# Attention steps of 256 queries inside the first MLP, with TensorE held to the source's order from block 1 on

## The chip, the cores and the metric

One NeuronCore of a Trainium2 chip runs the whole kernel. The metric is the device time of one execution in microseconds (us); of the kernel before three executions were timed, and one more was profiled. TensorE (PE in the profile) does the matmuls, VectorE (DVE) and ScalarE (ACT) the element-wise work, and SyncE's queue (SP) issues every DMA.

## What is computed

Chunked attention feeds two MLPs (called "moe" in the reference, with no routing):

```python
# attention: 4 batches, 8 heads, 768 queries, head size 64; per chunk of 32 queries
k_full = concat([mem_k (8), k[c_start-16 : c_end+8]])      # at most 64 keys
scores = q_c @ k_full.T / sqrt(64)
a = exp(scores - max(scores));  a = a / (sum(a) + 1e-9)
out_c = a @ v_full
# MLP 1 on x = out as [3072 tokens, 512]
h = x @ w_in;   y = (h * sigmoid(1.702 * h)) @ w_out        # 512 -> 2048 -> 512
# MLP 2 on y
h = y @ w_in2;  result = (max(h,0) + alpha * min(h,0)) @ w_out2
```

## The kernel before, in words

The 3,072 tokens are cut into 24 **attention steps** of 128 queries (`m` = 0 to 23). One step loads q, k and v (lines 273 to 285), forms the scores on TensorE (`sc`, L295: 32 small matmuls, which the trace counts as 64, in two PSUM banks of which half is used), then does the softmax: the row maximum and the subtraction on VectorE (L316, L324), the exponential on ScalarE (L337), the sum, reciprocal and scaling on VectorE (L343 to L348). Four transposes (`pt`, L358) turn the probabilities, ScalarE copies them out (L363), 32 matmuls with v give the step's output (`xp`, L373, again 64 in the trace), and ScalarE and VectorE split it into a high and a low part of `x` (L387, L388). For `m` in `NACC` (4 to 7) the exponential is eight ScalarE instructions with a running sum (L332) in place of one.

MLP 1 runs over six blocks of 512 tokens, in each over 16 chunks of 128 hidden units. Every product is made of three matmuls on high and low parts. One **MLP step** is `mm1` (L425: 12 matmuls 128x512 into `h`, of which there are two buffers), the activation on ScalarE and VectorE (L433, L434), its split into `gh` and `gl` (L470, L471), and one MLP step later `mm2` (L481: 12 matmuls into the pairs `ya` and `yb`, one buffer each). At a block's end `finish1` copies the four banks out (L490, L492) and stores them. During block 0 the 16 chunks of weights are converted from a 64-bit format (lines 108 to 144: about 4.6 us of VectorE each, and two ScalarE passes). From the sixth MLP step of block 1 on, the weights of MLP 2 are prepared on the side (`prep_place`, lines 192 to 239: per unit four VectorE passes over 1024 columns, four small sums L221, three subtractions L233, and casts on ScalarE).

Steps 0 to 3 run ahead of block 0. Steps 4 to 23 are spread over blocks 0 to 4 by `plan`: step `m` starts at tick `8*(m-4)`; its transposes stand three ticks later, the product with v five. Two ticks belong to an MLP step (`attend`, lines 823 to 826). The four parts of a step share one place of two PSUM banks, tag `"a"`. A scheduler then sorts the instructions of each engine by its own estimate of when they are ready; only those passed to `keep_in_program_order` (`kp`) stay where the source has them. TensorE's MLP 1 and attention instructions are free before the change. An engine takes its instructions one after another in the sorted order. Later stages (MLP 2, L621 and L719) are in fixed order and untouched.

Of the kernel before, what the change touches and what calls it, by code (L numbers as in the profile page):

```python
# [17 lines left out]
QG = 64  # L18
WIN = LEFT + CHUNK + RIGHT
NK = NMEM + LEFT + QG + RIGHT + NMEM  # L20
KW = NMEM + WIN
# [37 lines left out]
def fused_kernel(ctx: ExitStack, tc: tile.TileContext, qs, ks, vs, ident, w_in1, w_out1, w_in2, w_out2, alpha, out):  # L59
# [210 lines left out]
    def pair(tag, name):  # L270
        return ps1.tile([128, 2, DM], F32, tag=tag, name=name)
# [107 lines left out]
    def a_xcopy(m):  # L379
# [7 lines left out]
        nc.scalar.copy(hi, x)  # L387
        nc.vector.tensor_tensor(out=lo, in0=x, in1=hi.bitcast(F32), op=ALU.subtract)  # L388

    plan = {}  # L390
# [28 lines left out]
    def mm1(p, x, n, f):  # L419
        h = ps2.tile([128, TBM], F32, tag="h", name=f"h{p}")  # L420
        wh, wl = wt[p, f]
        i = 0
        for k in range(NKC):
            for w, z in ((wh, 0), (wh, 1), (wl, 0)):
                nc.tensor.matmul(  # L425
                    h[:, :n], w[:, 0, k * 128:(k + 1) * 128], x[:, z, k, :n], start=(i == 0), stop=(i == 3 * NKC - 1)
                )
                i += 1
        return h

# [45 lines left out]
    def mm2_t(p, y, gs, n, f):  # L476
        gh, gl = gs
        wh, wl = wt[p, f]
        for m in range(NKC):
            for i, (w, g) in enumerate(((wh, gh), (wh, gl), (wl, gh))):  # L480
                nc.tensor.matmul(  # L481
                    y[m][:, :n], w[:, 1, m * 128:(m + 1) * 128], g[:, :n],
                    start=(f == 0 and i == 0), stop=(f == NF - 1 and i == 2),
                )

    def finish1(y, t0, n):
        for m in range(NKC):
# [323 lines left out]
    a_load(NSTART)  # L811
    a_load_v(NSTART)

    def do_mm2(i):
        p, j, t0, n, f = steps[i]
# [98 lines left out]
```

## Time and profile before

| | us |
|---|---|
| median of 3 runs (1100.96 to 1103.57) | 1101.12 |
| the profiled execution, its own time | 1100.41 |
| span of its trace | 1098.6 |
| TensorE busy | 1070.5 (97% of the span) |
| VectorE busy | 766.3 (70%) |
| ScalarE busy | 409.7 (37%) |

Matmuls are pipelined: in a stream of 128x512 matmuls each has a duration of 0.39 us, but the next starts about 0.227 us after it. In what follows a **slot** is that distance from one start to the next, and the cost of something put between two big matmuls is what it adds to the sum of slots.

### The profile page before, as it was taken

What the parts mean: (1) busy time and instruction counts of PE and PEld (TensorE: products, weight loads), DVE (VectorE), ACT (ScalarE), POOL (GpSimd) and SP (SyncE); (2) the same over time, 40 slices, a digit from 0 to 9 for tenths busy, and PEclk for the clock granted to TensorE, in tenths of its full rate; (3) what the DMA queues carried; (4) which work ended last, traced back from release to release, by engine and by line L of the source; (5) the groups of instructions that cost most, each with busy time, mean ns of one, the idle gap of its engine ahead of it and who ended that gap; (6) DMA issues with size and microseconds to landing.
All of it is one profiled execution on the core that took longest, in us unless ns stands there. A gap on an engine that the chain in (4) does not pass through costs nothing.

```text
span 1098.6 us, 18378 instructions
## 1 busy us (share of the span) xinstructions
PE 1070.5 (97%) x7516; PEld 867.9 (79%) x7516; DVE 766.3 (70%) x1090; ACT 409.7 (37%) x633; POOL 0.2 (0%) x4
## 2 busy tenths in 40 slices
PE   5799999999999999999999999999999999999998
PEld 4577778888887887788788888888888888888886
DVE  6899833667676767766652257898777888677965
ACT  2566523334434434434432222245222345122442
POOL 0000000000000000000000000000000000000000
PEclk6699999999999999999999999999999999999999
DMA  8763522446646554665432066676666867666661
GB/s 292 261 202 125 158 84 64 151 170 217 219 165 208 192 194 151 222 215 177 158 130 67 1 194 197 210 268 207 201 199 199 296 200 216 201 187 212 219 203 58
DMA packets 84098, 200.23 MB, mean 182 GB/s; under 512 B 9520, under 2 KB 26288, under 8 KB 84016
## 3 DMA queue, kind: packets, MB, share of 16 engines
q1 hardware_dynamic: 84016, 199.07, 55.7%
q8 instruction: 59, 0.97, 0.4%
q14 instruction: 23, 0.19, 0.1%
HBM read 157.10 MB, written 41.94 MB: 181 GB/s over the span
## 4 chain that ended last, share of the span: by engine, by line
PE 87%; DVE 6%; DMA 3%; ACT 2%; issue 1%; SPq 0%; DVEq 0%; ACTq 0%
PE h L425 21%; PE accx L719 15%; PE accx L621 12%; PE ya L481 11%; PE yb L481 10%; PE accy L719 6%; PE accy L621 6%; PE hz L621 3%; PE xp L373 2%; DMA wraw<-w_out 2%; PE sc L295 1%; DVE wtmp L127 1%; DVE wtmp L124 1%; PE pt L358 1%; DMA y<-o 1%
## 5 line engine op out<-in xcount | busy, mean ns | idle before, releaser
L425 PE MATMUL h<-x,whi 128*128 128x512 f32 x768 | 246.0, 396 | 3.8 <-ACT whi L137 1.8
L425 PEld LDWEIGHTS h<-x,whi 128*128 128x128 f32 x768 | 143.6, 189 | 36.3 <-ACT whi L137 2.6
L434 DVE SCALAR_TENSOR_TENSOR t<-t,h 128x512 f32<-128x512 f32 x96 | 65.8, 685 | 125.8 <-ACT t L433 125.6
L425 PE MATMUL h<-x,wlo 128*128 128x512 f32 x384 | 152.0, 396 | 0.0
L433 ACT ACTIVATE t<-h 128x512 f32<-128x512 f32 x96 | 57.6, 600 | 162.8 <-PE h L425 162.6
L719 PE MATMUL accx<-r,u 128*128 128x512 f32 x360 | 86.5, 395 | 0.0
L621 PE MATMUL accx<-xw,u 128*128 128x512 f32 x240 | 85.7, 390 | 0.2 <-ACT u L604 0.2
L425 PEld LDWEIGHTS h<-x,wlo 128*128 128x128 f32 x384 | 72.4, 188 | 15.6 <-DVE wlo L142 0.4
L719 PE MATMUL accx<-rx,u 128*128 128x512 f32 x360 | 84.6, 390 | 0.0
L471 DVE TENSOR_TENSOR gl<-t,gh 128x512 fp32r<-128x512 f32 x96 | 65.8, 686 | 23.0 <-ACT gh L470 21.8
L719 PEld LDWEIGHTS accx<-r,u 128*128 128x128 f32 x360 | 67.5, 187 | 16.3
L719 PEld LDWEIGHTS accx<-rx,u 128*128 128x128 f32 x360 | 67.3, 188 | 15.0 <-DVE rx L674 0.5
L470 ACT CAST gh<-t 128x512 fp32r<-128x512 f32 x96 | 59.7, 622 | 45.9 <-DVE t L434 41.6
L481 PE MATMUL ya<-gh,whi 128*128 128x512 f32 x192 | 76.2, 397 | 0.3 <-ACT gh L470 0.3
L481 PE MATMUL ya<-gl,whi 128*128 128x512 f32 x192 | 76.3, 397 | 0.0
L481 PE MATMUL yb<-gl,whi 128*128 128x512 f32 x192 | 75.3, 392 | 0.0
L481 PE MATMUL yb<-gh,wlo 128*128 128x512 f32 x192 | 75.3, 392 | 0.0
L481 PE MATMUL yb<-gh,whi 128*128 128x512 f32 x192 | 75.1, 391 | 0.0
L481 PE MATMUL ya<-gh,wlo 128*128 128x512 f32 x192 | 75.1, 391 | 0.0
L604 ACT COPY s<-accx 128x512 f32<-128x512 f32 x24 | 14.1, 589 | 148.4 <-PE accx L621 148.4
L670 ACT CAST rx<-g 128x1024 fp32r<-128x1024 f32 x42 | 44.4, 1057 | 64.7 <-DVE g L454 24.3
L621 PE MATMUL accx<-xh,u 128*128 128x512 f32 x192 | 66.9, 389 | 0.0
(130 smaller groups left out, 1818.4 us busy)
## 6 DMA issues: line engine op xcount, KB each, us to landing
u<-wo SPq DMA_DIRECT2D x84, 512.0 KB, 4.7
u<-wi SPq DMA_DIRECT2D x72, 512.0 KB, 4.2
v<-vs SPq DMA_DIRECT2D x24, 512.0 KB, 4.3
k<-ks SPq DMA_DIRECT2D x24, 416.0 KB, 5.1
wraw<-w_in SPq DMA_DIRECT2D x16, 512.0 KB, 5.2
wraw<-w_out SPq DMA_DIRECT2D x16, 512.0 KB, 5.8
raw<-w_in SPq DMA_DIRECT2D x32, 256.0 KB, 3.6
wi<-ob SPq DMA_DIRECT2D x16, 512.0 KB, 4.0
```

Source lines behind the costliest of these rows:

```text
L124: nc.vector.scalar_tensor_tensor(out=a, in0=top, scalar=0xC0000000, in1=a, op0=ALU.bitwise_and, op1=ALU.bitwise_or)
L373: nc.tensor.matmul(x[half[z], g, j, c * CHUNK:(c + 1) * CHUNK], s["v"][half[g], c, 2 * j + z, :], s["p"][half[g], 2 * z + j // 2, b * CHUN ...
L425: nc.tensor.matmul(h[:, :n], w[:, 0, k * 128:(k + 1) * 128], x[:, z, k, :n], start=(i == 0), stop=(i == 3 * NKC - 1))
L433: mark["s"] = nc.scalar.activation(out=t[:, :n], in_=h[:, :n], func=AF.Tanh, scale=1.702 / 2).ins
L434: mark["v"] = nc.vector.scalar_tensor_tensor(out=t[:, :n], in0=t[:, :n], scalar=1.0, in1=h[:, :n], op0=ALU.add, op1=ALU.mult).ins
L470: mark["s"] = nc.scalar.copy(gh[:, :n], g[:, :n]).ins
L471: mark["v"] = lo_eng.tensor_tensor(out=gl[:, :n], in0=g[:, :n], in1=gh[:, :n].bitcast(F32), op=ALU.subtract).ins
L481: nc.tensor.matmul(y[m][:, :n], w[:, 1, m * 128:(m + 1) * 128], g[:, :n], start=(f == 0 and i == 0), stop=(f == NF - 1 and i == 2),)
L604: kp(nc.scalar.copy(t, src))
L621: kp(nc.tensor.matmul(to, w[:, c, k * 128:(k + 1) * 128], x[:, k], start=(i == 0 and n not in ADDED), stop=(i == 5), skip_group_check=n in ...
L670: kp(nc.scalar.copy(ring[P, d, jj][0], src))
L719: kp(nc.tensor.matmul(to[:, m], w[:, ft, c, m * 128:(m + 1) * 128], g[:, ft], start=(jj == 0 and ft == 0 and i == 0 and n not in ADDED), s ...
```

## The change

From step 4 on, two steps are taken together (`m` = 4, 6, ... 22): ten double steps of 256 queries with functions of their own, `d_load` to `d_xcopy`. Scores, transposed probabilities and outputs now fill both banks of the place `"a"`. The row maximum, subtraction, sum, scaling and the copy of the probabilities work on 1024 columns at once; the exponential for `m` in `NACC` (now 4 and 6) is 16 ScalarE instructions. The three loads are twice as large and are planned together five ticks ahead. The probabilities `p` share the SBUF place of q (tag `qp`) and the exponentials that of k (tag `ke`), one buffer each. A double step starts every 16 ticks, transposes five ticks and the product with v eight ticks after the start. From the first step of block 1 on, `pe()` keeps TensorE's instructions of MLP 1 and attention in the source's order.

```diff
+    def pe(i):
+        if pinned:
+            tc.keep_in_program_order(i)
...
+    def d_load(m):
+        q = ap["pool"].tile([128, 2, 2, 2, HP, CHUNK], F32, tag="qp", name=f"q{m}")
+        nc.sync.dma_start(out=q.rearrange("p s g c j q -> p s (g c j q)"), in_=qs[m:m + 2].rearrange("s p n -> p s n"))
+        k = ap["pool"].tile([128, 2, 2, HP, NK], F32, tag="ke", name=f"k{m}")
+        nc.sync.dma_start(out=k.rearrange("p s g j n -> p s (g j n)"), in_=ks[m:m + 2].rearrange("s p n -> p s n"))
+        v = ap["pool"].tile([128, 2, 2, H, D], F32, tag="v", name=f"v{m}")
+        nc.sync.dma_start(out=v.rearrange("p s c h d -> p s (c h d)"), in_=vs[m:m + 2].rearrange("s p n -> p s n"))
...
+        nc.vector.tensor_reduce(out=mx, in_=flat(sc), axis=mybir.AxisListType.X, op=ALU.max)
...
+        nc.vector.tensor_tensor(out=flat(ex), in0=flat(sc), in1=over(mx), op=ALU.subtract)
...
+            for i in range(DW):
+                nc.scalar.activation(
+                    out=ex[:, i], in_=sc[:, i], func=AF.Exp, scale=1.0 / D ** 0.5,
+                    bias=t["nmx"][:, i:i + 1], accum_out=sm[:, i:i + 1],
+                )
...
+        nc.vector.tensor_tensor(out=ex, in0=ex, in1=over(sm), op=ALU.mult)
...
+        t["p"] = ap["pool"].tile([128, 2, 4, 128], F32, tag="qp", name=f"p{m}")
...
-    for m in range(NSTART, NSG):
+    for m in range(NSTART, NSG, 2):
         b = 8 * (m - NSTART)
         if m > NSTART:
-            at(b - 7, a_load, m)
-            at(b - 2, a_load_v, m)
-        at(b, a_scores, m)
-        at(b, a_max, m)
-        at(b, a_exp, m)
-        at(b + 1, a_norm, m)
-        at(b + 3, a_trans, m)
-        at(b + 3, a_pcopy, m)
-        at(b + 5, a_pv, m)
-        at(b + 5, a_xcopy, m)
-    done_tick = lambda m: 0 if m < NSTART else 8 * (m - NSTART) + 6
+            at(b - 5, d_load, m)
+        at(b, d_scores, m)
+        at(b, d_max, m)
+        at(b, d_exp, m)
+        at(b + 2, d_norm, m)
+        at(b + 5, d_trans, m)
+        at(b + 5, d_pcopy, m)
+        at(b + 8, d_pv, m)
+        at(b + 8, d_xcopy, m)
+    done_tick = lambda m: 0 if m < NSTART else 8 * ((m - NSTART) // 2 * 2) + 9
...
-                nc.tensor.matmul(
+                pe(nc.tensor.matmul(
...
+        if i == NF:
+            pinned.append(True)
```

How the change moves instructions, at three places. First **TensorE at the end of block 0 and in block 2**, the scores of a step (`sc`) among the big matmuls (`h` is mm1, `ya` and `yb` are mm2). Before, the scores of step 8, in pieces of 3, 1 and 28:

```order
L425 MATMUL h_1614<-x_738,wlo_0_339 128x512
L295 MATMUL sc_1660<-k_1440,q_1438 32x64 x3
L481 MATMUL ya<-gh,whi_15_1353 128x512
L481 MATMUL yb<-gh,whi_15_1353 128x512
L295 MATMUL sc_1660<-k_1440,q_1438 32x64
L481 MATMUL ya<-gl,whi_15_1353 128x512
```

In the change, the scores of the double step 12 (L417), between a whole mm1 (now L545) and a whole mm2 (now L601):

```order
L545 MATMUL h_2628<-x_1970,whi_3_667 128x512 x2
L545 MATMUL h_2628<-x_1970,wlo_3_668 128x512
L417 MATMUL sc_2650<-k_2549,q_2547 32x64 x64
L601 MATMUL ya<-gh,whi_2_545 128x512
L601 MATMUL ya<-gl,whi_2_545 128x512
L601 MATMUL ya<-gh,wlo_2_546 128x512
```

In blocks 1 to 5 TensorE now alternates 12 matmuls of mm1 and 12 of mm2, and each part of a double step stands in one piece between two of these groups; in each of the eight double steps there, two mm1 and two mm2 stand between the scores and the transposes.

Second, **VectorE in block 2**, the softmax of step 12 among the activation (`t`, `gl`) and the preparation (`oa`, `ob`). Before:

```order
L316 TENSOR_REDUCE mx_2670<-sc_2635 128x8
L324 TENSOR_TENSOR ex_2671<-sc_2635,mx_2670 128x512
L434 SCALAR_TENSOR_TENSOR t<-t,h_2676 128x512
L233 TENSOR_TENSOR ob_2_2594<-ob_2_2594 128x2x256
L233 TENSOR_TENSOR ob_2_2595<-ob_2_2595 128x2x256
L343 TENSOR_REDUCE sm_2674<-ex_2671 128x8
L471 TENSOR_TENSOR gl<-t,gh 128x512
L346 TENSOR_SCALAR sm_2674<-sm_2674 128x8
L347 RECIPROCAL sm_2674<-sm_2674 128x8
L348 TENSOR_TENSOR ex_2671<-ex_2671,sm_2674 128x512
```

In the change (L441 is the maximum, L446 the subtraction, L466 the sum, L469 the scaling, L554 and L591 the activation):

```order
L441 TENSOR_REDUCE mx_2717<-sc_2650 128x16
L446 TENSOR_TENSOR ex_2718<-sc_2650,mx_2717 128x1024
L466 TENSOR_REDUCE sm_2721<-ex_2718 128x16
L554 SCALAR_TENSOR_TENSOR t<-t,h_2750 128x512
L233 TENSOR_TENSOR oa_2577<-oa_2577 128x3x256
L467 TENSOR_SCALAR sm_2721<-sm_2721 128x16
L591 TENSOR_TENSOR gl<-t,gh 128x512
L233 TENSOR_TENSOR ob_3_2728<-ob_3_2728 128x2x256
L233 TENSOR_TENSOR ob_3_2729<-ob_3_2729 128x2x256
L468 RECIPROCAL sm_2721<-sm_2721 128x16
L469 TENSOR_TENSOR ex_2718<-ex_2718,sm_2721 128x1024
L554 SCALAR_TENSOR_TENSOR t<-t,h_2791 128x512
```

The softmax instructions are half as many and twice as wide, and the three subtractions of the preparation (L233) and one whole activation stand between the sum and the scaling.

Third, **ScalarE at the start of block 0**: the cast of step 3's output (`x_267<-xp_487`), for which the first mm1 waits, and the exponentials of step 4. Before:

```order
L363 COPY p_485<-pt_480 128x512
L322 ACTIVATE nmx_600<-mx_597 128x8
L332 ACTIVATE ex_598,sm_602<-sc_564,nmx_600 128x64 x8
L387 CAST x_267<-xp_487 128x2x4x64
L110 ACTIVATE wtmp<-wraw_2_329 128x1024
```

In the change:

```order
L363 COPY p_485<-pt_480 128x512
L387 CAST x_267<-xp_487 128x2x4x64
L110 ACTIVATE wtmp<-wraw_2_329 128x1024
L110 ACTIVATE wtmp<-wraw_3_429 128x1024
L444 ACTIVATE nmx_634<-mx_631 128x16
L455 ACTIVATE ex_632,sm_636<-sc_564,nmx_634 128x64 x13
L553 ACTIVATE t<-h_548 128x512
```

The cast now stands ahead of the exponentials, and these ahead of the first activation.

## Rows read from the trace of the kernel before

**Rows 1.** Windows: span, busy of PE, PEld, DVE, ACT, POOL; PEclk, DMA, GB/s

```profile
150.00:250.00 100.00, 100.00 (x970) 80.93 (x948) 56.94 (x95) 35.26 (x58) 0.00 (x0) 1.00 0.39 131
```

**Rows 2.** Timeline of TensorE, step 9 in block 1: start, duration, instruction

```profile
171.20 0.39 PE L425 MATMUL h<-x,wlo 128*128 128x512 f32 x1
...
172.56 0.39 PE L481 MATMUL ya<-gh,wlo 128*128 128x512 f32 x1
172.87 0.86 PE L295 MATMUL sc<-k,q 64*32 64x64 f32 x64
173.66 0.50 PE L481 MATMUL yb<-gh,whi 128*128 128x512 f32 x1
174.00 0.39 PE L481 MATMUL yb<-gl,whi 128*128 128x512 f32 x1
...
182.41 0.39 PE L425 MATMUL h<-x,wlo 128*128 128x512 f32 x1
182.64 0.60 PE L358 MATMUL pt<-id_sb,ex 128*128 128x128 f32 x4
182.99 0.71 PE L425 MATMUL h<-x,whi 128*128 128x512 f32 x2
...
187.86 0.39 PE L425 MATMUL h<-x,whi 128*128 128x512 f32 x1
188.17 1.14 PE L373 MATMUL xp<-p,v 64*64 64x32 f32 x64
189.24 0.50 PE L425 MATMUL h<-x,whi 128*128 128x512 f32 x1
```

**Rows 3.** Timeline of TensorE, a piece of six score matmuls in step 8

```profile
145.78 0.39 PE L425 MATMUL h<-x,wlo 128*128 128x512 f32 x1
146.10 0.31 PE L295 MATMUL sc<-k,q 64*32 64x64 f32 x6
146.34 0.50 PE L481 MATMUL ya<-gh,whi 128*128 128x512 f32 x1
```

**Rows 4.** Waits of TensorE, 150 to 545 us: total us, times, longest

```profile
PE h L425 <- DVE t L434: 0.7, 1, 0.7
PE h L425 <- ACT x L387: 0.7, 1, 0.7
PE h L425 <- DVE x L388: 0.6, 1, 0.6
```

**Rows 5.** Timeline of VectorE, softmax of step 9 (no preparation beside it)

```profile
172.31 0.69 DVE L434 SCALAR_TENSOR_TENSOR t<-t,h 128x512 f32<-128x512 f32 x1 [3.90 <-ACT t L433]
173.69 0.69 DVE L471 TENSOR_TENSOR gl<-t,gh 128x512 fp32r<-128x512 f32 x1 [0.69 <-ACT gh L470]
174.30 0.68 DVE L316 TENSOR_REDUCE mx<-sc 128x8 f32<-128x512 f32 x1
...
176.41 0.69 DVE L343 TENSOR_REDUCE sm<-ex 128x8 f32<-128x512 f32 x1 [0.70 <-ACT ex L337]
...
177.57 0.69 DVE L348 TENSOR_TENSOR ex<-ex,sm 128x512 f32<-128x512 f32 x1
```

**Rows 6.** Groups of instructions on VectorE: busy us, mean ns of one, idle before

```profile
L124 DVE SCALAR_TENSOR_TENSOR wtmp<-wraw,wtmp 128x1024 uint32<-128x1024 uint32 x16 | 19.5, 1218 | 0.0
...
L233 DVE TENSOR_TENSOR oa<-oa 128x768 fp32r<-128x768 f32 x16 | 15.2, 953 | 0.2
...
L221 DVE TENSOR_TENSOR ob<-oa 128x256 f32<-128x256 f32 x32 | 12.1, 418 | 0.0
```

**Rows 7.** Chain of waits: the exponentials of step 4 ahead of block 0

```profile
36.59 2.49 ACT ex L332 x15
```

**Rows 8.** Timeline of TensorE: its longest wait in block 0

```profile
126.81 0.73 PE L425 MATMUL h<-x,whi 128*128 128x512 f32 x2 [1.84 <-ACT whi L137]
```

**Rows 9.** DMA rate over the first 25 us, in 40 slices

```profile
GB/s 0 0 26 210 365 373 370 301 257 218 306 305 357 361 394 403 412 424 403 424 407 396 397 419 402 399 392 393 340 209 131 37 26 92 138 367 229 131 265 365
```

**Rows 10.** Timeline of ScalarE: the last copy out of `yb` at a block's end

```profile
448.77 0.60 ACT L490 ACTIVATE o<-yb 128x512 f32<-128x512 f32 x1 [5.30 <-DMA y<-o]
```

More of the change, by code (lines that the diff above doesn't have):

```diff
@@ L388, in a_xcopy @@
         nc.vector.tensor_tensor(out=lo, in0=x, in1=hi.bitcast(F32), op=ALU.subtract)
+    DW = 2 * HP * 2
+    pinned = []
+    def pe(i):
[8 more added lines that the diff above has]
+        nc.sync.dma_start(out=v.rearrange("p s c h d -> p s (c h d)"), in_=vs[m:m + 2].rearrange("s p n -> p s n"))
+        st[m] = dict(q=q, k=k, v=v)
@@ new lines, in d_scores @@
+    def d_scores(m):
+        t = st[m]
+        sc = pair("a", f"sc{m}").rearrange("p z (s n k) -> p z s n k", s=2, k=KW)
+        for s in range(2):
+            for jh in range(2):
+                for g in range(2):
+                    for c in range(2):
+                        for jp in range(2):
+                            for z in range(2):
+                                pe(nc.tensor.matmul(
+                                    sc[quarter[2 * c + jp], z, s, 2 * jh + g, :], t["q"][half[z], s, g, c, 2 * jh + jp, :],
+                                    t["k"][half[z], s, g, 2 * jh + jp, run[c]], start=True, stop=True,
+                                ))
+        t["sc"] = sc
@@ new lines, in flat, with over, d_max @@
+    def flat(t):
+        return t.rearrange("p z s n k -> p (z s n) k")
+    def over(t):
+        return t.rearrange("p (n k) -> p n k", k=1).to_broadcast([128, DW, KW])
+    def d_max(m):
+        t = st[m]
+        sc = t["sc"]
+        for s in range(2):
+            for g in range(2):
+                for n in (g, 2 + g):
+                    if (2 * (m + s) + g) % GPB == 0:
+                        nc.vector.memset(sc[half[0], :, s, n, NMEM:NMEM + LEFT], NEG)
+                    if (2 * (m + s) + g) % GPB == GPB - 1:
+                        nc.vector.memset(sc[half[1], :, s, n, WIN - RIGHT:WIN], NEG)
+        mx = ap["pool"].tile([128, DW], F32, tag="mx", name=f"mx{m}")
+        t["ex"] = ex = ap["pool"].tile([128, 2, 2, 4, KW], F32, tag="ke", name=f"ex{m}")
+        nc.vector.tensor_reduce(out=mx, in_=flat(sc), axis=mybir.AxisListType.X, op=ALU.max)
+        if m in NACC:
+            t["nmx"] = ap["pool"].tile([128, DW], F32, tag="nmx", name=f"nmx{m}")
+            nc.scalar.mul(t["nmx"], mx, -1.0 / D ** 0.5)
+            return
+        nc.vector.tensor_tensor(out=flat(ex), in0=flat(sc), in1=over(mx), op=ALU.subtract)
@@ new lines, in d_exp @@
+    def d_exp(m):
+        t = st[m]
+        ex = flat(t["ex"])
+        t["sm"] = sm = ap["pool"].tile([128, DW], F32, tag="sm", name=f"sm{m}")
+        if m in NACC:
+            sc = flat(t["sc"])
+            for i in range(DW):
[3 more added lines that the diff above has]
+                )
+            return
+        nc.scalar.activation(out=ex, in_=ex, func=AF.Exp, scale=1.0 / D ** 0.5)
@@ new lines, in d_norm, with d_trans @@
+    def d_norm(m):
+        t = st[m]
+        ex, sm = flat(t["ex"]), t["sm"]
+        if m not in NACC:
+            nc.vector.tensor_reduce(out=sm, in_=ex, axis=mybir.AxisListType.X, op=ALU.add)
+        nc.vector.tensor_scalar(out=sm, in0=sm, scalar1=1e-9, scalar2=None, op0=ALU.add)
+        nc.vector.reciprocal(sm, sm)
+        nc.vector.tensor_tensor(out=ex, in0=ex, in1=over(sm), op=ALU.mult)
+    def d_trans(m):
+        t = st[m]
+        t["pt"] = pt = pair("a", f"pt{m}").rearrange("p s (i q) -> p s i q", q=128)
+        e = t["ex"].rearrange("p z s (j g) k -> p z s j (g k)", g=2)
+        for s in range(2):
+            for i in range(4):
+                pe(nc.tensor.transpose(pt[:, s, i, :], e[:, i // 2, s, i % 2, :], id_sb))
@@ new lines, in d_pcopy, with d_pv @@
+    def d_pcopy(m):
+        t = st[m]
+        t["p"] = ap["pool"].tile([128, 2, 4, 128], F32, tag="qp", name=f"p{m}")
+        nc.scalar.copy(t["p"], t["pt"])
+    def d_pv(m):
+        t = st[m]
+        x = pair("a", f"xp{m}").rearrange("p g (s j q) -> p g s j q", s=2, q=QG)
+        for s in range(2):
+            for j in range(HP):
+                for c in range(2):
+                    b = 2 * c + j % 2
+                    for g in range(2):
+                        for z in range(2):
+                            pe(nc.tensor.matmul(
+                                x[half[z], g, s, j, c * CHUNK:(c + 1) * CHUNK], t["v"][half[g], s, c, 2 * j + z, :],
+                                t["p"][half[g], s, 2 * z + j // 2, b * CHUNK:(b + 1) * CHUNK], start=True, stop=True,
+                            ))
+        t["x"] = x
@@ new lines, in d_xcopy @@
+    def d_xcopy(m):
+        tok = m * SQ
+        b = int(np.searchsorted(p1_start, tok, side="right")) - 1
+        if b not in xt:
+            xt[b] = xp.tile([128, 2, NKC, TBM], F32R, tag=f"x{b % 2}", name=f"x{b}")
+        x = st.pop(m)["x"]
+        for s in range(2):
+            off = tok + s * SQ - int(p1_start[b])
+            hi, lo = [xt[b][:, i, :, off:off + SQ].rearrange("p j (g q) -> p g j q", g=2) for i in range(2)]
+            nc.scalar.copy(hi, x[:, :, s])
+            nc.vector.tensor_tensor(out=lo, in0=x[:, :, s], in1=hi.bitcast(F32), op=ALU.subtract)
@@ L424, in mm1 @@
             for w, z in ((wh, 0), (wh, 1), (wl, 0)):
-                nc.tensor.matmul(
+                pe(nc.tensor.matmul(
                     h[:, :n], w[:, 0, k * 128:(k + 1) * 128], x[:, z, k, :n], start=(i == 0), stop=(i == 3 * NKC - 1)
-                )
+                ))
                 i += 1
```

7 lines of the change are left out of this document (3 added, 4 removed).

## The prediction

> **What bounds the kernel now.** I read the windows by stage first: in block 1 TensorE is busy for all of its 100 us at the full granted clock (1.00, the level of 2.4 GHz), VectorE for 57 and ScalarE for 35 [rows 1]. So in MLP 1 time is saved only by shortening what TensorE does or by removing what it waits for. Then TensorE's timeline, to see what an attention step costs there. A big matmul starts 0.227 us after the one before it. The slot after 172.56 would begin at 172.79; the scores put it off to 173.66, and the matmul after that comes 0.34 us later, not 0.23: 0.87 + 0.11 = 0.98 us for 64 matmuls. The four transposes cost in the same way 182.99 - 182.64 = 0.35, with the 0.11 behind them 0.46; the product with v 189.24 - 188.09 + 0.11 = 1.26 [rows 2]. One step: 2.70 us, two: 5.40. A piece of only six score matmuls costs 146.34 - 146.01 + 0.11 = 0.44 [rows 3]. So 58 further matmuls cost 0.54 us, 9 ns each, and a piece has a fixed part of 0.44 - 6 x 0.009 = 0.38 us. That is what larger steps can save. Last the waits: between 150 and 545 us TensorE waits only three times, 2.0 us in all [rows 4].
>
> The sum is made against the profiled execution, 1100.41 us; the median of the runs shown lies 0.71 above it.
>
> **Blocks 1 to 4, larger pieces: -8.0 us.** Eight double steps. Scores 0.98 + 64 x 0.009 = 1.56; transposes with the same fixed part 0.38 + 2 x 0.08 = 0.54; product with v 0.38 + 2 x 0.88 = 2.14. Together 4.24, which saves 1.16 us per double step. If only the 0.11 behind a piece were fixed, three pieces less would save 0.33. I take 1.0, near the first, because the piece of six is measured for the scores alone: 8 x 1.0, bounds 2.6 and 9.3.
>
> The Trainium skill states in "TensorE: Matmul & The Clock Gate", section "Wait — 56ns, not 53.3ns?", that start to start never falls below about 25 ns, however small a matmul is. The trace disagrees for these matmuls (9 ns each), and the measurement decides. By the rule the 128 matmuls added to scores and output would cost an estimated 3.2 us instead of 1.5, a double step some 6.0 in place of 5.4, and this term would be +4.6.
>
> **Source order, no cut pieces: -1.9 us.** Before, the scores of steps 8, 12 and 16 are cut into three, two and three pieces; five pieces less by 0.38.
>
> **Source order, waits of before: -2.0 us.** The three waits [rows 4] come from mm1 matmuls that the scheduler put ahead of what they need, two of them at the start of block 5, where `x` came late. In source order the last product with v of a block stands two MLP steps ahead of the block's end, so `x` is there. Bounds 0 and 2.6, the latter if the slow restart after a wait goes too.
>
> **Source order, waits at the transposes: +9.3 us.** This is the term that eats the others. From the scores' end TensorE has two mm1 and two mm2 before the transposes: 48 slots, 10.9 us. In that time VectorE must finish a softmax twice as wide, among the instructions that the scheduler puts between. I count from the end of the slot of the last mm1 matmul (t = 0; at 171.43 in step 9). The activation's VectorE part starts at 0.88, `gl` at 2.26 [rows 5]. Queued instructions of 0.69 us start 0.61 apart [rows 5], so a pass over 1024 columns, 1.22 alone [rows 6], counts 1.13 in a queue and 1.25 where the next one needs its result. The exponential takes about 0.70 of the 2.11 us between maximum and sum [rows 5]; twice as wide I estimate 1.1.
>
> Step 12, as the order of the change has it: activation 0.88 to 1.48, a preparation pass to 2.61, `gl` to 3.2, four L221 (0.42 alone [rows 6], 0.35 in a queue) with two memsets to 4.8, maximum 6.05, subtraction 7.3, exponential 8.4, sum 9.55, next activation 10.15, the wide L233 (0.95 [rows 6]) 11.05, the small addition 11.25, `gl` 11.85, two L233 of 0.6 each 13.05, reciprocal 13.25, scaling 14.5; transposes at 14.65. TensorE gets there at 1.6 + 0.1 + 10.9 = 12.6. It waits 2.1 us. The same count gives 1.5 for step 14, 2.1 for 16 and for 18 (two preparation passes between), 0.6 for 20 and 0.9 for 22. Steps 8 and 10, with little or no preparation beside them, are ready at 9.5 to 11: no wait. Sum 9.3. Bounds: 0, if the preparation falls elsewhere (step 9 alone took 178.26 - 174.30 = 4 us from maximum to scaling, twice as wide it would be under 7), and 14, if each of the six waits is 0.8 us longer. `gl` is late too, but needed only behind the transposes; the copy of `p` and the product with v come 8.2 us after the transposes and hide a wide ScalarE copy.
>
> **Block boundaries: +1.3 us.** In source order the next block's first matmul into `yb` stands 18 slots (4.1 us) after the last mm2. At the end of block 3 ScalarE has the activation of the mm1 between (done at 2.7 + 0.85) and a preparation pass (about 1.2) ahead of the last copy out of `yb` (0.6): 5.4, a wait of 1.3. Elsewhere the copy stands earlier. Bounds: 0, and 8, if the longest wait for a store's buffer, 5.3 us [rows 10], came at each of four boundaries with 2 us of it uncovered.
>
> **Start and block 0: -2.0 us.** The cast of step 3's output no longer stands behind the exponentials of step 4, which took 2.5 us ahead of the first mm1 [rows 7]; but the weights that come next are converted no earlier, so most of that head start ends in a wait. Steps 5's scores move into the time ahead of block 0, where TensorE waits anyway, and the pieces of the others come out about level with before (still cut, since block 0 is not pinned): 1 to 1.5 us. VectorE, close to full here, saves about 1 us on wider instructions. Against it: the loads of step 5 (q, k, v of 1.2 MB) now stand ahead of those of steps 2 and 3 on SyncE's queue. At some 400 GB/s that is 3 us, mostly taken up by the pause near 20 us, where the rate falls to 26 GB/s [rows 9]: 0.5 us remain. And 16 exponentials in a row hold ScalarE for 4.7 us, twice; before, eight of them went ahead of a cast of weights for which TensorE waited 1.84 us [rows 8]. Bounds -4 and +6.
>
> At nothing: the later loads, three of twice the size in place of six. k waits for the transposes of the step before, q and v for its product with v, and behind them on SyncE's queue stand the preparation's loads and the stores of y; but they are planned five ticks ahead of the scores, some 15 us (a block of 100 us has 32 ticks). If that cover went, the scores would wait for a landing of about 5 us.
>
> Sum: -8.0 - 1.9 - 2.0 + 9.3 + 1.3 - 2.0 = -3.3. That makes 1097.1 for the profiled execution and **1097.8** as a median: faster by 3.3 us, 0.3%. A measurement of this kernel can tell about 0.3% (3.3 us) from no change, so the likeliest case lies on that line.
>
> **Rivals.** *A: the transposes come in time.* For it: VectorE is busy only 57 to 70% in these blocks, and a wait at one step lets its queue catch up. Against: the instructions between are in its fixed order. Price: 9.3 us less, 1088.5. *B, slower: ScalarE's 16 exponentials.* If each of the two bunches makes TensorE wait for casts of weights as in [rows 8], longer by the 2.3 us that eight more exponentials take, block 0 has two waits of 4.1 us in place of one of 1.84: +6.4, and the -2.0 goes: 1106.2. It decides if the casts behind the exponentials are those of the chunk that TensorE needs next; the order puts a bunch directly ahead of the casts of chunks 2 and 3, and of chunk 13. Against: TensorE has products of earlier chunks left to fill in. *C: larger pieces are no cheaper*, so the change doesn't do what its size says: 1097.8 + 8 = 1105.8, or about 1110 if each added matmul took the rule's floor. Rows 3 speak against it.
>
> **How the numbers follow.** Forecast 0.50 (its own range 1094 to 1102, from the bounds of the waits taken half each way), A 0.23, B 0.20, C 0.07. Faster by over 0.3%: nearly half of the forecast and all of A, 0.47. Within: half of the forecast and a part of B, where only one bunch hurts, 0.33. Slower: the rest of B, C, and the forecast with the boundaries at their worst, 0.20. The range 1089 to 1106 takes in most of A and B.
>
> **What would show it.** Scores, transposes and product at about 1.6, 0.6 and 2.1 us of slots; waits of TensorE for the scaling (now L469) in six of the ten double steps, 1 to 2 us each, none in steps 8 and 10; no wait for `x` at the start of block 5; block 0 shorter by about 2 us with one wait for a cast of weights. The prediction is wrong if L469 is no releaser of TensorE, if block 0 is longer than before, or if the granted clock falls below 1.00 around those waits.

## The result, and the profile after

The change made the kernel slower: 1109.26 us as a median of six runs (1107.85 to 1113.52), against 1101.13 of the kernel before on the same chip. The ratio is 1.0073, 95% interval 1.0054 to 1.0092. The prediction was 1097.8, with a range up to 1106. The profiled execution took 1108.17 us (span 1106.4), 7.8 us more than that of before. One execution of the kernel of experiment 8 took 3,733 us; it is left out of the ratio and the median given there.

The windows by stage of the changed kernel first, for blocks 1, 2 and 3 (columns as in [rows 1]):

```profile
150.00:250.00 100.00, 100.00 (x927) 82.56 (x926) 56.77 (x85) 36.12 (x55) 0.00 (x0) 1.00 0.38 130
250.00:350.00 100.00, 96.88 (x905) 79.49 (x904) 64.06 (x100) 39.40 (x59) 0.00 (x0) 0.98 0.55 193
350.00:450.00 100.00, 96.12 (x902) 78.82 (x901) 66.87 (x104) 37.91 (x58) 0.00 (x0) 0.98 0.51 179
```

The last two of the kernel before:

```profile
250.00:350.00 100.00, 100.00 (x917) 80.60 (x916) 69.12 (x115) 40.74 (x65) 0.00 (x0) 1.00 0.58 197
350.00:450.00 100.00, 99.96 (x919) 80.86 (x918) 66.29 (x115) 39.21 (x64) 0.00 (x0) 1.00 0.55 189
```

In block 1 TensorE is as full as in [rows 1]. In blocks 2 and 3 it idles 3 to 4 us in every hundred, where it was full before, and the granted clock falls from 1.00 to 0.98. VectorE is no fuller than before (64 and 67 us against 69 and 66). TensorE's waits from 150 to 545 us, beside [rows 4]:

```profile
PE pt L477 <- DVE ex L469: 8.3, 6, 1.9
PE yb L601 <- ACT o L610: 0.9, 1, 0.9
```

The three waits of before are gone. Six waits of the transposes for the scaling have come, 8.3 us. The longest one on TensorE's timeline, step 12:

```profile
262.21 1.49 PE L417 MATMUL sc<-k,q 64*32 64x64 f32 x128
...
274.42 0.39 PE L545 MATMUL h<-x,wlo 128*128 128x512 f32 x1
276.75 1.74 PE L477 MATMUL pt<-id_sb,ex 128*128 128x128 f32 x8 [1.95 <-DVE ex L469]
278.14 0.78 PE L601 MATMUL ya<-gh,whi 128*128 128x512 f32 x1
278.72 0.63 PE L601 MATMUL ya<-gl,whi 128*128 128x512 f32 x1
279.14 0.63 PE L601 MATMUL ya<-gh,wlo 128*128 128x512 f32 x1
...
280.42 0.40 PE L601 MATMUL ya<-gh,wlo 128*128 128x512 f32 x1
```

The scores are one piece of 128, as planned. Behind the wait the transposes take 1.74 us, and five big matmuls start 0.42 to 0.58 us behind the one before instead of 0.23. The window there shows why:

```profile
276.70:280.40 3.70, 3.65 (x13) 3.22 (x14) 2.39 (x4) 2.66 (x3) 0.00 (x0) 0.54 0.80 252
```

The granted clock is 0.54: nearly all of that stretch ran at the lower level, 1.2 GHz. From 280.40 us on it is 1.00 again. The same came behind the wait of step 16 (0.55 from 379.00 to 382.60 us). The five slots from 278.14 to 280.42 take 2.28 us instead of 5 x 0.227, the six of step 16 (379.88 to 382.58) 2.70 instead of 1.36: 2.5 us together.

VectorE in that wait, beside [rows 5]:

```profile
266.95 1.22 DVE L441 TENSOR_REDUCE mx<-sc 128x16 f32<-128x1024 f32 x1
268.21 1.22 DVE L446 TENSOR_TENSOR ex<-sc,mx 128x1024 f32<-128x1024 f32 x1
270.62 1.22 DVE L466 TENSOR_REDUCE sm<-ex 128x16 f32<-128x1024 f32 x1 [1.19 <-ACT ex L460]
271.75 0.68 DVE L554 SCALAR_TENSOR_TENSOR t<-t,h 128x512 f32<-128x512 f32 x1
272.35 0.95 DVE L233 TENSOR_TENSOR oa<-oa 128x768 fp32r<-128x768 f32 x1
...
273.90 1.28 DVE L233 TENSOR_TENSOR ob<-ob 128x512 fp32r<-128x512 f32 x2
...
275.38 1.22 DVE L469 TENSOR_TENSOR ex<-ex,sm 128x1024 f32<-128x1024 f32 x1
```

It is busy from the maximum to the scaling but for 1.19 us, in which it waits for the exponential. The preparation stands in the middle of the softmax.

Block 0 is longer too. VectorE copies `ya` out at 150.43 us, before at 148.70. TensorE, then ScalarE (the accumulator reads between the exponentials are left out), then VectorE at the first MLP steps:

```profile
47.59 0.39 PE L545 MATMUL h<-x,wlo 128*128 128x512 f32 x1
50.61 1.51 PE L545 MATMUL h<-x,whi 128*128 128x512 f32 x4 [2.62 <-DVE sm L467]
...
43.19 0.31 ACT L455 ACTIVATE ex<-sc,nmx 128x64 f32<-128x64 f32 x1
...
46.68 0.38 ACT L455 ACTIVATE ex<-sc,nmx 128x64 f32<-128x64 f32 x1
...
46.97 0.67 ACT L553 ACTIVATE t<-h 128x512 f32<-128x512 f32 x1
...
47.50 2.36 DVE L127 SCALAR_TENSOR_TENSOR wtmp<-wraw,wtmp 128x1024 uint32<-128x1024 uint32 x2
49.77 0.68 DVE L554 SCALAR_TENSOR_TENSOR t<-t,h 128x512 f32<-128x512 f32 x1
50.37 0.17 DVE L467 TENSOR_SCALAR sm<-sm 128x16 f32<-128x16 f32 x1
```

Thirteen exponentials of step 4 stand ahead of the first activation. VectorE fills the time with conversions, takes the activation's second part at 49.77, and TensorE stands still for 2.62 us. The row of that wait names L467, the small instruction right behind the activation in VectorE's queue; what the next mm1 needs is the `h` that L554 reads. Before, eight such exponentials had run ahead of the first mm1 [rows 7].

### The profile page after: what moved, and what is told of

The parts are those of the page before. It is cut to its first block, busy times and chain, and to the rows that moved or that the text cites. A ratio compares the mean times of both kernels' runs of the same rounds, so it can differ in the third digit from the quotient of the medians.

```text
span 1106.4 us, 18264 instructions
## 1 busy us (share of the span) xinstructions
PE 1069.2 (97%) x7516; PEld 872.2 (79%) x7516; DVE 759.0 (69%) x1034; ACT 407.0 (37%) x613; POOL 0.2 (0%) x4
## 4 chain that ended last, share of the span: by engine, by line
PE 81%; DVE 10%; DMA 4%; ACT 2%; issue 2%; SPq 0%; DVEq 0%; ACTq 0%
PE h L545 17%; PE accx L839 15%; PE accx L741 12%; PE ya L601 9%; PE yb L601 9%; PE accy L839 6%; PE accy L741 6%; PE hz L741 3%; PE xp L493 2%; DMA k<-ks 1%; PE pt L477 1%; DVE ex L469 1%; DVE gl L591 1%; DVE wtmp L124 1%; DVE wtmp L127 1%
## 5 line engine op out<-in xcount | busy, mean ns | idle before, releaser
L545 PE MATMUL h<-x,whi 128*128 128x512 f32 x768 | 241.7, 396 | 3.4 <-DVE sm L467 2.6
L545 PEld LDWEIGHTS h<-x,whi 128*128 128x128 f32 x768 | 144.7, 190 | 35.8 <-ACT whi L137 3.4
L554 DVE SCALAR_TENSOR_TENSOR t<-t,h 128x512 f32<-128x512 f32 x96 | 65.7, 685 | 150.2 <-ACT t L553 150.2
L545 PE MATMUL h<-x,wlo 128*128 128x512 f32 x384 | 151.0, 394 | 0.0
L545 PEld LDWEIGHTS h<-x,wlo 128*128 128x128 f32 x384 | 72.9, 190 | 15.8
L591 DVE TENSOR_TENSOR gl<-t,gh 128x512 fp32r<-128x512 f32 x96 | 65.8, 686 | 27.3 <-ACT gh L590 27.3
L601 PE MATMUL ya<-gh,whi 128*128 128x512 f32 x192 | 78.4, 408 | 1.5 <-ACT gh L590 1.4
L601 PE MATMUL ya<-gl,whi 128*128 128x512 f32 x192 | 76.7, 399 | 1.1 <-DVE gl L591 1.1
L601 PE MATMUL yb<-gh,whi 128*128 128x512 f32 x192 | 75.4, 393 | 0.9 <-ACT o L610 0.9
L601 PE MATMUL ya<-gh,wlo 128*128 128x512 f32 x192 | 75.9, 395 | 0.0
L601 PE MATMUL yb<-gh,wlo 128*128 128x512 f32 x192 | 75.0, 391 | 0.0
L601 PE MATMUL yb<-gl,whi 128*128 128x512 f32 x192 | 74.9, 390 | 0.0
```

Source lines behind the costliest of these rows:

```text
L545: pe(nc.tensor.matmul(h[:, :n], w[:, 0, k * 128:(k + 1) * 128], x[:, z, k, :n], start=(i == 0), stop=(i == 3 * NKC - 1)))
L554: mark["v"] = nc.vector.scalar_tensor_tensor(out=t[:, :n], in0=t[:, :n], scalar=1.0, in1=h[:, :n], op0=ALU.add, op1=ALU.mult).ins
L591: mark["v"] = lo_eng.tensor_tensor(out=gl[:, :n], in0=g[:, :n], in1=gh[:, :n].bitcast(F32), op=ALU.subtract).ins
L601: pe(nc.tensor.matmul(y[m][:, :n], w[:, 1, m * 128:(m + 1) * 128], g[:, :n], start=(f == 0 and i == 0), stop=(f == NF - 1 and i == 2),))
```

## The experiments

The theory at the outset (W): the loss is TensorE's waits for the scaling, with the lower clock level behind two of them, and a wait at the start of block 0. The rivals: source order costs by itself; VectorE as a whole is too full; larger pieces bring nothing. The letters of later rivals are explained in the expectations. In the diffs `...` stands for lines left out. Ratios are to the kernel before on the same chip.

**1. Transposes and product two ticks later, from step 8 on.**

```diff
+        z = 2 if m >= 8 else 0
-        at(b + 5, d_trans, m)
-        at(b + 5, d_pcopy, m)
-        at(b + 8, d_pv, m)
-        at(b + 8, d_xcopy, m)
+        at(b + 5 + z, d_trans, m)
+        at(b + 5 + z, d_pcopy, m)
+        at(b + 8 + z, d_pv, m)
+        at(b + 8 + z, d_xcopy, m)
...
```

> Edit: the changed kernel, but from step 8 on the transposes, the copy of the probabilities, the product with v and its copy stand two ticks (one MLP step) later: 72 big matmuls between scores and transposes instead of 48, 16.3 us instead of 10.9. Theory W (the changed kernel loses by TensorE's waits for the scaling, L469, and by the half-speed stretches behind two of them): seen from the changed kernel, the transposes of steps 12 to 22 cost 10.2 us more than the 0.79 us that they cost without a wait, and the half-speed stretches near 278 and 380 us cost 2.8 us; the longest wait was 1.95 us, so 5.4 us more room ends all of them: 1109.3 - 13 = 1096, TensorE never waits for L469 between 150 and 545 us, and the granted clock is 1.00 from 250 to 450 us. Rival S (TensorE waits because VectorE's queue as a whole is too full beside the preparation; a wait that is removed comes back at another place, at the split of the activation or at the next scores): at most half of it is won, 1103 or more, with new waits of TensorE for VectorE of 1 us and over.

Measured: 1099.37 us, ratio 0.9987 (0.9974 to 1.0000), 10 us less than the change. The waits from 150 to 545 us and the windows:

```profile
PE yb L602 <- ACT o L611: 0.9, 1, 0.9
PE ya L602 <- DVE gl L592: 0.8, 2, 0.6
PE ya L602 <- ACT gh L591: 0.7, 1, 0.7
```

```profile
250.00:350.00 100.00, 98.76 (x918) 80.67 (x917) 67.52 (x104) 41.41 (x62) 0.00 (x0) 1.00 0.56 198
350.00:450.00 100.00, 99.78 (x925) 81.89 (x924) 70.34 (x109) 40.24 (x62) 0.00 (x0) 1.00 0.56 196
```

No wait for the scaling is left, the clock is 1.00, and VectorE does the same work without being late. That is W, with two corrections of size. Small waits for `gl` and `gh` of 1.5 us came in place, and in that trace the wait at 47 us was 3.5 us instead of 2.6: 10 us instead of 13.

**2. The change without source order.**

```diff
-        if i == NF:
-            pinned.append(True)
```

> Edit: the changed kernel without the line that starts to hold TensorE to the source's order at block 1. Theory W (waits for the scaling at the transposes are the loss; source order itself is a gain, because it leaves each part of a double step in one piece): in the order that the scheduler makes, the transposes still stand 45 to 60 big matmuls behind most scores, so most waits stay, and the scores of blocks 1 to 4 are cut into some 29 pieces instead of 8, the products with v into some 15 instead of 8; 28 pieces more by 0.33 to 0.38 us are 9 to 10 us: about 1117, bounds 1110 and 1120. Rival P (being held to the source's order is what costs): 1105 or less.

Measured: 1105.81 us, ratio 1.0040 (1.0027 to 1.0053): neither forecast. TensorE waits for nothing between 150 and 545 us. Summed over TensorE's timeline, the 52 attention pieces there cost 43.5 us where the 24 whole ones of experiment 1 cost 35.1: 8.4 us for 28 pieces more, and 11.5 with the 0.11 behind each, where I had 9 to 10. So the price of the extra pieces was about right, but I was wrong that the waits would stay: the scheduler puts the transposes of steps 12 to 16 68 to 72 big matmuls behind the scores instead of 48. (Step 18 keeps 48, and still has 1.2 us in hand where the change waited 1.94, so VectorE's order differs as well.) The time from the scaling's end to the transposes shows it, in us, for the double steps 8, 10, ... 22:

| kernel | 8 | 10 | 12 | 14 | 16 | 18 | 20 | 22 |
|---|---|---|---|---|---|---|---|---|
| the change | 3.0 | 1.8 | 0.15 | 0.15 | 0.14 | 0.15 | 0.15 | 0.15 |
| without source order | 2.9 | 2.1 | 3.3 | 3.3 | 3.3 | 1.2 | 3.9 | 3.4 |
| two ticks later | 9.3 | 4.6 | 3.2 | 7.8 | 6.2 | 7.4 | 4.9 | 4.5 |

Where it reads 0.15 the transposes started as soon as they could. In the kernel before, 15 of 16 single steps have 4.1 to 4.9 us in hand (2.4 the other): the scheduler had kept that reserve, and source order took it away.

**3. Source order with the single steps of the kernel before.**

```diff
-                            nc.tensor.matmul(
+                            pe(nc.tensor.matmul(
...
+        if i == NF:
+            pinned.append(True)
```

(`pe` around the five places of TensorE's matmuls and transposes in attention, mm1 and mm2.)

> Edit: the kernel before (steps of 128 queries), with TensorE held to the source's order from block 1 on, as in the change. Theory W: single steps need half the VectorE time between scores and transposes, and 36 big matmuls (8.2 us) stand there; no waits at the transposes over 0.5 us, five cut pieces less (1.9 us), and the three waits of before go (2.0 us), against about 1 us at the blocks' ends: 1101.1 - 3 = 1098, bounds 1096 and 1101. Rival P (source order costs by itself, at the blocks' ends and where the scheduler moved matmuls out of the way of a late operand): 1104 or more.

Measured: 1104.30 us, ratio 1.0030 (1.0019 to 1.0042): W fell here, P's number came. The waits from 150 to 545 us:

```profile
PE pt L364 <- DVE ex L354: 3.5, 3, 2.1
PE yb L487 <- ACT o L496: 1.2, 1, 1.2
```

So small steps wait as well once their places are fixed, here 36 big matmuls behind the scores: one for 2.1 us (with the clock at the lower level behind it), two for 0.6 and 0.8. The size of the steps is not the cause by itself; a fixed place with too little room for that size is. Whether source order costs as such stayed open, for experiments 7 and 8.

**4. Single steps beside block 0, double steps from step 8 on.** The list of block 0 is that of the kernel before, and the SBUF place is opened anew at block 1.

```diff
-    for m in range(NSTART, NSG, 2):
+    for m in range(NSTART, 8):
...
+    for m in range(8, NSG, 2):
+        b = 8 * (m - NSTART) + (2 if m == 8 else 0)
+        at(b - 5 + (m == 8), d_load, m)
...
+            att.close()
+            att_open("at2", 1)
```

> Edit: the changed kernel with steps 4 to 7 (those beside block 0) as single steps as in the kernel before; double steps from step 8 on, step 8 two ticks later so that its loads, which need the SBUF place of the single steps, have four ticks. Theory W with its second part (block 0 lost about 1.7 us against before, because 13 of the 16 exponentials of step 4 stand on ScalarE ahead of the activation of the first mm1 matmuls, and TensorE waits 2.6 us at 47.6 us and then runs at the half level until 54.7 us): block 0 ends as in the kernel before, 1.7 us earlier, first mm1 at 41.1 us, no wait of TensorE for L467: 1109.3 - 1.7 = 1107.6, 1 us more if step 8, now beside the first preparation units, waits at its transposes. Rival L (block 0 is longer for another reason, as the larger loads ahead of those of the first steps): the scores' wait for k near 10 us is back to 7.9 us from 8.8 and the first mm1 starts earlier than in the kernel before, but the wait for L467 has nothing to do with it; the same 1.7 us or less. Told apart by where the time comes back, before or after the first mm1.

Measured: 1102.80 us, ratio 1.0018 (1.0009 to 1.0027): 6.5 us less than the change instead of 1.7. The first mm1 of block 1 starts at 142.79 us in the trace, in the change at 146.10, though the first mm1 of all is 1.25 us later (41.23 against 39.98); no wait for L467. So these 3.3 us came back behind the first mm1, which is W's place and not L's, and they are twice its size. The rest of the span took 2.8 us less: step 22 doesn't wait here (0.9), and only one half-speed stretch came where the change had two, which no edit here aimed at.

**5. Both edits, 1 and 4.** The diff is that of 4 and that of 1, the latter with

```diff
-        z = 2 if m >= 8 else 0
+        z = 2 if m >= 10 else 0
```

> Edit: the two earlier edits together: single steps beside block 0 as in the kernel before, double steps from step 8 on (step 8 two ticks later), and from step 10 on the transposes and the product with v two ticks later. Theory W (two separate losses: the waits at the transposes, and block 0): the first edit alone gave a trace whose blocks 1 to 4 took 392.8 us (150.2 to 543.0), the second one whose block 1 began at 145.5 us instead of 150.2; they touch different places, so both are won: 1099.4 - 4.7 = 1094.7, bounds 1093 and 1097, faster than both kernels. Rival R (a gain in block 0 is given back, because an earlier block 1 meets the same deadlines of VectorE's preparation or of loads): 1098 or more, with waits of TensorE for VectorE or a DMA between 150 and 545 us that the first edit alone does not have.

Measured: 1096.10 us, ratio 0.9953 (0.9938 to 0.9967). Both gains add, as W said: the 9.9 us of experiment 1 and the 3.3 of block 0 make 13.2, and 13.2 came. It is faster than either kernel.

**6. What the start waits for.** First the exponentials behind the first activation:

```diff
+                with tc.issue_after(mark["s"]):
-                nc.scalar.activation(
+                    nc.scalar.activation(
```

> Edit: the changed kernel, but the 16 exponentials of steps 4 and 6 are issued only behind the activation of the MLP step at whose place they stand; on ScalarE the activation of the first mm1 now stands ahead of the exponentials, where 13 of them stood ahead of it. Nothing else in the source changes. Theory X (the exponentials ahead of the first activation are what makes TensorE wait 2.6 us at 47.6 us): the first activation starts near 45.2 us, when its mm1 is done, instead of 46.97, the wait shrinks to under 1 us, and block 1 starts 2 us earlier: 1107. Rival V (VectorE's conversions are the limit there: its part of the activation stood behind two conversion passes that ended at 49.9 us): the wait stays within 0.7 us of 2.6, or the second activation, now behind all 16 exponentials, makes a new one of 2 us and over: 1109 or more.

Measured: 1110.17 us, ratio 1.0089 (1.0074 to 1.0104). The activation ran ahead of the exponentials, and its cast `gh` then stood behind all 16: TensorE waits 3.4 us for L591 in place of 2.6 for L467. V's number came, but the new wait is ScalarE's. Then one wide exponential for step 4 in place of the 16:

```diff
-NACC = (4, 5, 6, 7)
+NACC = (6,)
```

> Edit: the changed kernel with step 4 out of the list of steps whose exponential runs in pieces: its 16 exponentials become one of 128x1024, and VectorE subtracts the maximum and forms the sum (about 1.2 us each). ScalarE has some 3.6 us less to do at the first mm1, VectorE some 2.4 us more. Theory X' (the ScalarE time of the 16 exponentials is what TensorE waits for at the start, at the activation or at its cast, wherever they are put): the waits of 2.6 us (as it is) and of 3.4 us (with the exponentials behind the first activation) shrink to under 1.5 us, block 1 starts 1.5 to 2.5 us earlier, 1107.3. Rival V' (VectorE, with 13 conversion passes in the first 10 us of block 0, is the limit there): the wait stays over 2 us or is split, 1109 or more.

Measured: 1105.35 us, ratio 1.0035 (1.0023 to 1.0047), 3.9 us less than the change; X' had forecast 2 us less. In the traces, 3.1 us apart, only 1.0 us of it lies ahead of block 1; 1.6 us lie in block 2, where the clock did not fall behind step 12 in that trace. So X' holds for the direction, not for the wait: it is still 2.61 us, now for `gl` on VectorE, where the sum of step 4 stands ahead of it:

```profile
50.72 1.21 DVE L466 TENSOR_REDUCE sm<-ex 128x16 f32<-128x1024 f32 x1
51.85 0.68 DVE L591 TENSOR_TENSOR gl<-t,gh 128x512 fp32r<-128x512 f32 x1
```

A double step brings more work there than either engine has room for: on ScalarE, or, moved over, on VectorE. And all exponentials as one instruction each, in the kernel of experiment 1:

```diff
-NACC = (4, 5, 6, 7)
+NACC = ()
```

> Edit: the changed kernel with the transposes and the product with v two ticks later from step 8 on (as run already, 1099.4), and with every exponential as one instruction (steps 4 and 6 too). If theory X' holds for both bunches of 16: block 0 is 2 to 3.5 us shorter (the wait at 47 us of 3.5 us in that trace, and the one of 1.4 us for the cast near 113 us): 1096.5, bounds 1095 and 1098, about level with single steps beside block 0 (1096.1). Rival V' (VectorE is the limit of block 0): 1099 or more.

Measured: 1097.58 us, ratio 0.9965 (0.9952 to 0.9978), 1.8 us less than experiment 1 and within the bounds of X' (1095 to 1098). But its reason holds in part only: block 1 begins 1.2 us earlier in the trace, not 2 to 3.5, and the start still has a wait of 2.6 us for `gl`.

**7. Single steps in source order, with room: transposes and product one tick later.**

```diff
-        at(b + 3, a_trans, m)
...
-        at(b + 5, a_pv, m)
...
-    done_tick = lambda m: 0 if m < NSTART else 8 * (m - NSTART) + 6
+        z = 1 if m >= 8 else 0
+        at(b + 3 + z, a_trans, m)
...
+        at(b + 5 + z, a_pv, m)
...
+    done_tick = lambda m: 0 if m < NSTART else 8 * (m - NSTART) + (7 if m >= 8 else 6)
```

(The two copies move along.)

> Edit: the kernel before with TensorE held to the source's order from block 1 on (as run already), and from step 8 on the transposes, the product with v and their copies one tick later: 48 big matmuls between scores and transposes instead of 36, 10.9 us instead of 8.2. Theory W' (source order costs only where its fixed places are too tight; the scheduler of the kernel before moved the transposes of a late step back by itself): the waits at the transposes between 145 and 545 us (3.5 us in three places, about 5.5 with the slow restart behind them) go, those at the blocks' ends (2.8 us) stay: 1104.3 - 5.5 = 1098.8, bounds 1097 and 1101. Rival Q (source order costs as such): 1102 or more; also if the product with v, now 12 or 24 matmuls ahead of the next scores, makes these wait for the place in PSUM, 0.5 to 2 us each.

Measured: 1112.90 us, ratio 1.0109 (1.0090 to 1.0127), the slowest of all. The waits from 150 to 545 us:

```profile
PE yb L488 <- ACT o L497: 3.7, 2, 3.2
PE sc L301 <- DVE x L394: 3.3, 6, 1.0
PE pt L364 <- DVE ex L354: 2.4, 2, 2.1
```

The product now stands so close ahead of the next scores that these wait for the place in PSUM, which VectorE still reads for the low part of `x`. It was Q's second clause. The wait of 3.2 us is for ScalarE's last copy out of `yb` at the end of block 3, which itself waited 1.38 us for a store to free its buffer. And the edit did not give every step the 48 big matmuls that were expected: the ticks of a block are spread up to `done_tick`, which moved too, and in the trace the transposes of steps 9 to 11 still stand 36 big matmuls behind the scores; the wait of 2.1 us is that of step 11, as in experiment 3. So this run tells nothing of source order as such, and the product went back to its place:

**8. The same with the transposes and their copy alone one tick later.** Against experiment 7:

```diff
-        at(b + 5 + z, a_pv, m)
-        at(b + 5 + z, a_xcopy, m)
+        at(b + 5, a_pv, m)
+        at(b + 5, a_xcopy, m)
```

> Edit: the kernel before with TensorE held to the source's order from block 1 on, and from step 8 on only the transposes and their copy one tick later (48 big matmuls behind the scores instead of 36); the product with v stays, 12 big matmuls behind the transposes and 24 to 36 ahead of the next scores. The run that moved the product too made the scores wait for the place in PSUM (3.3 us in six places) and the last copy of a block come late (3.2 us in one), so it could not tell what source order costs by itself. Theory W' (only too tight places cost): no wait of the scores, waits at the transposes under 0.5 us in blocks 1 to 4, 1104.3 - 5.5 + 0.5 = 1099, bounds 1097 and 1101. Rival Q (with steps of 128 queries source order costs as such: there are twice as many places where TensorE can stand still): 1102 or more, with new waits at the product with v or at the blocks' ends.

Measured: 1099.30 us, ratio 0.9983 (0.9973 to 0.9993): W'. All steps from 8 on have 48 big matmuls between scores and transposes here. Source order with room is a little faster than the scheduler's order, also for single steps; and the 48 that are enough for a single step are too few for a double one. Run again for a trace:

> The same kernel as the one with single steps, source order and the transposes alone one tick later, once more for a trace (the profiled execution of that run took 3.7 ms and is no guide). Theory W' (doubles gain where nothing waits): the kernel with double steps from step 8 on and room (1096.1) was 3.4 us faster than this one (1099.5), and a double step costs 0.7 to 0.76 us less than two single ones, 5.6 to 6 us for eight; so this trace has no more waits than that one, and its 48 pieces in blocks 1 to 4 cost about 38.5 us without the slots behind them, where the 24 large ones cost 35.1. Rival: its waits alone (over 2 us more than in the trace with double steps) make the 3.4 us.

Measured: 1099.81 us (a single run). From 150 to 545 us one wait is left, of 1.0 us, for ScalarE's copy out of `yb`.

Summed over the timeline, its 48 pieces cost 38.3 us, the 24 of the double steps 35.1; the slot behind a piece costs 0.11 more, 24 x 0.11 = 2.6. So eight double steps save 5.8 us, 0.73 each; of these, 3.2 show in the medians of experiments 5 and 8. From the first mm1 to the last the two traces differ by 4.3 us; the trace of experiment 5 has more waits for `gl` and the copies, and its first mm1 is 1.9 us later.

**9. One tick instead of two in the version of experiment 5.**

```diff
-        z = 2 if m >= 10 else 0
+        z = 1 if m >= 10 else 0
```

> Edit: the fastest version so far (single steps beside block 0, transposes and product with v two ticks later from step 10 on, 1096.1) with one tick in place of two: from step 12 on 60 big matmuls (13.6 us) between scores and transposes, where the change has 48 and that version 72. The scaling ended 3.2 us or more ahead of the transposes there (3.2 us at step 12, least of all), and the longest wait in the change was 1.95 us; a tick is 2.72 us. Theory W: no wait for the scaling over 0.2 us, 1096, bounds 1094.5 and 1098. Rival M (the scheduler sets VectorE's order by its own estimate of when the transposes come, so room that is taken away is taken from the wait's side): waits for the scaling in two or more steps, 1 us each, 1099 or more.

Measured: 1093.68 us, ratio 0.9939 (0.9917 to 0.9961): 0.6% under the kernel before, and under W's bounds (1094.5 to 1098). The kernel before ran in 1099.82 on that chip, so the ratio tells more than the time, and its interval overlaps that of experiment 5: that one tick is better than two is not shown, only that it is no worse. The waits from 150 to 545 us:

```profile
PE ya L614 <- DVE gl L604: 1.5, 2, 0.9
PE yb L614 <- ACT o L623: 0.9, 1, 0.9
```

The scaling is never waited for; the smallest margin is 1.6 us, at steps 16 and 18. One tick of room (2.7 us) is enough where the longest wait was 1.95; rival M falls.

## Why the prediction was wrong

Its terms against the traces, in us:

| step of the prediction | predicted | measured |
|---|---|---|
| larger pieces | -8.0 | -5.6 |
| no cut pieces | -1.9 | -2.1 |
| waits of before gone | -2.0 | -2.0 |
| waits at the transposes | +9.3 | +8.3, with +4.4 behind them |
| block boundaries | +1.3 | +2.9 |
| start and block 0 | -2.0 | +1.7 |
| sum | -3.3 | +7.6; the traces differ by 7.8 |

The waits of before are idle time alone; the slots around them were 2.5 us too long. Block 0 is read by VectorE's copy of `ya`; by the first mm1 of block 1 (143.27 us before, 146.10 now) it ends 2.8 us later. So a row is good to about 1 us.

**Right: the mechanism, its places and its size.** The waits were to be 2.1, 1.5, 2.1, 2.1, 0.6 and 0.9 us at steps 12 to 22, and none at 8 and 10. Measured: 1.95, 1.17, 1.94, 1.94, 0.37 and 0.90, none at 8 and 10. Counting VectorE's queue in its order, with durations from the rows, gave each wait to 0.35 us. Experiment 1 shows that they, with what stands behind them, were the main loss, and experiment 9 that one tick of room is enough against them. Rival A fell by the same rows.

**Failed first: what stands behind a wait.** I priced the idle time alone. The transposes of those six steps cost 10.2 us more than six times the 0.79 that they cost without a wait, so 1.9 went into slow restarts, two of them at the lower clock level; and 2.5 us more went into the stretches at the lower clock level. That is the 4.4 us of the table, on a term that the sum had at nothing. The prediction named a granted clock under 1.00 around these waits as a sign that it would be wrong, and had put no price on it.

**Failed second: start and block 0**, wrong in sign. I held the later exponentials of step 4 for a gain, because they no longer delay the first mm1; it did start 1.1 us earlier. But they then delayed the first activation and cost 2.6 us of waiting and more time at the lower level: in the window from 50.60 to 54.80 us the granted clock is 0.63, where the kernel before has 0.99 from 44.50 to 60.00. Rival B had the engine and the two bunches right, and its casts of weights wrong: TensorE waited for an activation at 47.6 us and for `gh` at 112. Its price, 8.4 us on top of the forecast, was more than twice the 3.7 by which block 0 missed it. Its 1106.2, already just outside the range, held the waits at the transposes, but nothing for what stands behind them. The range allowed for one thing going wrong at a time; four terms were off the same way: behind the waits 4.4 us, start 3.7, larger pieces 2.4, boundaries 1.6.

**Failed third: the transposes' share of the larger pieces.** A double step costs 1.50 + 0.79 + 2.08 and three times the 0.11 behind a piece, 4.70 us, not the 4.24 worked out. Scores and product came within 0.05 us of my figures. The transposes cost 0.90 instead of 0.54: eight cost almost twice the 0.46 of four, so there is no fixed part to save, and the piece of six score matmuls [rows 3] was no guide to them. Rival C falls: a double step is 0.70 us cheaper than two single ones. 64 score records more cost 1.50 - 0.87 = 0.63 us, 10 ns each, and 64 of the product 2.08 - 1.15 = 0.93, 15 ns each. But the trace counts two records for every matmul that the source issues, and the prediction's 9 ns are per record; per matmul it is 20 ns for the scores and 29 for the product. The Trainium skill, "TensorE: Matmul & The Clock Gate", section "Wait — 56ns, not 53.3ns?", has a floor of about 25 ns from start to start. Per matmul of the source this trace doesn't agree for the scores and does for the product; per record it agrees for neither. By that floor the 64 matmuls added would cost an estimated 1.6 us, where the trace has 1.56, so the prediction's 3.2 came from counting records as matmuls.

**Block boundaries** cost twice the forecast. The wait at the end of block 3 was 0.89 us, 1.04 with its longer slot, against 1.3 predicted. But at the start of block 5, where the wait for `x` is gone as predicted, there are now two waits for `gl`, 1.1 us idle and 1.8 with the slots around them; these the prediction did not have.

## What to carry to other kernels

Holding an engine to the source's order makes its pieces whole, but it also takes away the reserve that a scheduler leaves ahead of a late operand. So count the producer's queue for every fixed place and give each at least the wait that the count shows. Price a wait of the busiest engine with its restart and its clock behind it (here half as much again), and let the range hold several terms off the same way, not one rival at a time.

## What the runs showed that was not expected

Waits of the same length do not always bring the clock down. In the change, it fell behind 1.95 us at step 12 and 1.94 at step 16, not behind 1.94 at step 18:

```profile
425.43 1.06 PE L477 MATMUL pt<-id_sb,ex 128*128 128x128 f32 x8 [1.94 <-DVE ex L469]
426.25 0.48 PE L601 MATMUL ya<-gh,whi 128*128 128x512 f32 x1
426.56 0.40 PE L601 MATMUL ya<-gl,whi 128*128 128x512 f32 x1
```

In experiment 4 it fell behind 1.93 us at step 16, not behind 1.95 and 1.97 at steps 12 and 18; in the second kernel of experiment 6 it fell behind 1.95 at step 16, not behind 1.95 and 1.96 at steps 12 and 18. What decides it was not tried. So some 1.5 us of a difference between two such kernels can be this alone.

The granted clock of the records can be wrong. In the trace of experiment 9 it reads 1.00 at the first mm1, yet these matmuls start 0.43 us apart, as they do in the kernel before, where it reads 0.50:

```profile
41.00:44.50 3.50, 3.50 (x11) 2.77 (x10) 3.46 (x5) 1.68 (x2) 0.00 (x0) 1.00 0.05 15
```

```profile
42.48 0.63 PE L558 MATMUL h<-x,wlo 128*128 128x512 f32 x1
42.90 1.05 PE L558 MATMUL h<-x,whi 128*128 128x512 f32 x2
43.76 0.62 PE L558 MATMUL h<-x,wlo 128*128 128x512 f32 x1
```

So a stretch is better judged by the distance of its matmuls than by that column alone.
